# Pooled attention and a softplus FFN on one core: two re-searched instruction orders, and fourteen identity products left out

## The chip, the cores and the metric

The kernel runs on one core of one Trainium2 chip. The metric is the device time of one execution in microseconds (us), as the median of several runs. The kernel of before has a median of 874.52 us over 3 runs (871.99, 874.52 and 875.28).

## What is computed

The reference, cut to what matters. All arrays are float32; B = 8 batches, H = 8 heads, S = 576 positions, D = 64; the FFN has 4608 tokens, 512 inputs and 2048 hidden values.

```python
k_p = k.reshape(B, H, S // 8, 8, D).mean(axis=3)      # keys and values pooled by 8
v_p = v.reshape(B, H, S // 8, 8, D).mean(axis=3)
scores = matmul(q, k_p^T) / sqrt(D);  scores -= max(scores)
attn = exp(scores) / sum(exp(scores))
x = matmul(attn, v_p)                                 # -> 4608 x 512
h = x @ w_in
g = maximum(h, 0) + log1p(exp(-abs(h)))               # softplus
out = g @ w_out
```

## The kernel before

The 4608 tokens are worked on in 18 chunks c of 256. Every float32 factor of the FFN is split into a rounded high part and a low rest, and a product is made of three passes (high by high, high by low, low by high), so TensorE is given three 128x256 products for one.

**Phase 1** (`ORDER1`) holds three chunks (0, 1, 2), the conversion of the 16 blocks of weights on VectorE (`weights`, its last step is L1016), and the pooling of the keys and values of batches 0 and 1 (`batch`). There, `keep_warm` (L313) puts extra products of an identity matrix by itself on TensorE: 3 and 4 in batch 0, 8 ahead of the keys of batch 1 (L1115), and 6 ahead of the transposes of the second q tile of chunk 2 (L360). They write into a bank that is written over afterwards. A 128x128 float32 product shows up as two records.

**Phase 2** (`ORDER2`) holds chunks 3 to 17 in a software pipeline. A chunk has eight blocks u. Steps of one block, with the short names that the text uses:

- **H c.u**: first FFN product, 24 products of 256 columns (L720). TensorE alternates: H c.u, M c.(u-1), H c.(u+1), M c.u, and so on.
- **softplus c.u** on ScalarE (L728), **rounded c.u** on ScalarE (L742), **low c.u** on VectorE (L749).
- From chunk 4 on the second product is made in a scheme of seven products for eight: **sums c.u** are four short operations on VectorE (L782 to L785), **sums-high c.u** on ScalarE (L796), **sums-low c.u** on VectorE (L801).
- **M c.u**: second FFN product, 21 products of 256 columns (L872), three for each of the seven outputs in the order 1, 2, 6, 7, 5, 3, 4. Blocks 0 and 7 have it in two parts of 12 and 9. The seven outputs lie in four PSUM banks, two to a bank; output 4 has half of the fourth bank, and **its three products are the last of every M**: 18 products stand ahead of them.

Steps of the attention of a chunk, which runs two chunks ahead of the FFN: **spread** (eight copies of q on ScalarE, L494), **scores c** (64 small products, L516), then on VectorE **least** (L538) and **less** (L554), on ScalarE **exp c** (L316), on VectorE **expsum** (L1355), **reciprocals** (L1359, L1360), **main** and **ends** (L1363), **turn** (L483), and on TensorE **values c** (L616, L627).

The scores of a chunk need a little more than two banks. From chunk 6 on, the last heads go into the half of the fourth bank of chunk c-2 that no output uses (`third_bank`, `ms[old]["rest"]`). The steps that read this half are called **third least** (L538, 128x144 in) and **third less** (L554, 128x144). They read chunk c's scores while M of chunk c-2 goes on writing output 4 into the other half of the same bank. The list of slots that `pair_scores` and `pair_least` are given names the bank; the M steps have no edge to these two readers in the list of steps.

The order is written out by hand as two lists of numbers of steps. `Order.run` hands out buffers in that order, and the steps are then issued in it: each engine runs its own steps in the order of the list, and where two steps on different engines touch the same tile, the one that stands later in the list waits for the one that stands earlier. ScalarE keeps one table of functions at a time; exponential and softplus are in different ones, and a load (ACT_TABLE_LOAD) stands where the function changes.

Of the kernel before, what the change touches and what calls it, by code (L numbers as in the profile page):

```python
# [69 lines left out]
def pooled_attention_softplus_ffn(  # L70
# [15 lines left out]
    POOL = 8  # L86
    SP = S // POOL
# [262 lines left out]
    def new_E(c):  # L350
        e_[c] = one.tile([P, T, H, SP], F32, tag="E", name="E")

    class Tile:
# [5 lines left out]
        def qT(self, ps):  # L359
            if (self.c, self.t) == (2, 1):  # L360
                keep_warm(ps, 6)
            for m in range(HP):
                nc.tensor.transpose(
                    out=ps[:, m * P:(m + 1) * P],
                    in_=qt_[self.c][:, self.t, 2 * m:2 * m + 2].rearrange("p h d -> p (h d)"),
                    identity=ident)
# [674 lines left out]
    def batch(b):  # L1041
# [60 lines left out]
        for i in range(2):  # L1102
# [10 lines left out]
            def products(i=i, N=N):  # L1113
                if i == 0:
                    keep_warm(bank(s_k, "kps"), (4, 8)[b])  # L1115
                ps = bank(s_k, "kps").rearrange("p (h d) -> p h d", h=H)
                for r in range(N):
                    nc.tensor.matmul(out=ps[0:KM, HP * i:HP * (i + 1)], lhsT=zm,
                                     rhs=x["k", i][:, :, r], start=r == 0, stop=r == N - 1)
            halves.append(op(PE, 0.1 + 0.28 * N, products, [o, *halves], [st[i], s_k]))  # L1120
# [27 lines left out]
    def attend(c):  # L1148
# [16 lines left out]
        for t, x in enumerate(tiles):  # L1165
# [12 lines left out]
            for i, s in enumerate(ss):  # L1178
                d = op(DVE, 0.37, lambda x=x, i=i, s=s, n=s_mn: x.least(i, s.tile, n.name), [p, *ends],
                       [s, s_mn])  # L1180
# [7 lines left out]
                ends.append(op(ACT, 1.18, exp_sum, [d], [s, s_mn, s_sm, s_E], table="exp"))  # L1188
# [153 lines left out]
    def probabilities(c, s_E, s_lt, subs, where):  # L1342
# [4 lines left out]
        if early:  # L1347
            ex = op(ACT, 1.1, lambda: exponential(e_[c]), subs, table="exp")
        else:
            ex = op(ACT, 1.1 + TABLE, lambda: exponential(e_[c]), [*subs, where], s_E)  # L1350
            op(ACT, TABLE, lambda: None, [ex], first=5000)
# [121 lines left out]
    for u in range(U1):  # L1473
# [60 lines left out]
    def first_products(c, u, before):  # L1534
# [16 lines left out]
        else:  # L1551
# [3 lines left out]
               first=HURRY)  # L1555
# [89 lines left out]
    for c in range(N1, NCH + 1):  # L1645
# [166 lines left out]
```

## Time and profile before

| | us |
|---|---|
| median of 3 runs | 874.52 |
| the profiled execution, as timed | 870.77 |
| its span (first to last instruction) | 868.8 |
| TensorE busy | 849.2 (98%) |
| VectorE busy | 661.4 (76%) |
| ScalarE busy | 524.4 (60%) |
| granted TensorE clock, mean | 0.998 |

In the rows, PE is TensorE, DVE VectorE, ACT ScalarE, SP the queue that issues DMAs. A matmul's record covers its way through a pipeline, so two records overlap and a busy PE need not be at its full rate; a row of the timeline gives start, length, and, in square brackets, how long the engine had been idle and what ended that. L numbers are lines of the kernel of before.

### The profile page before, as it was taken

The numbers are of one execution on the slowest core, as the hardware profiler recorded it, in microseconds if no ns is written. First come the engines' busy times: TensorE is split into PE (matmuls) and PEld (weight loads), VectorE is DVE, ScalarE is ACT, GpSimd is POOL, SyncE is SP. The second block draws the span as 40 slices with busy tenths as digits, with TensorE's granted clock in tenths as the row PEclk, the third lists the DMA queues.
The fourth block names the chain that finished last, engine by engine and source line by source line (L and its number), as shares of the span: only waits on it lengthen the run. The fifth ranks groups of instructions, "written<-read, shape, count | busy, mean of one in ns | idle before, by whom it ended". The sixth has DMA issues, their size and how long they took to land.

```text
span 868.8 us, 21296 instructions
## 1 busy us (share of the span) xinstructions
PE 849.2 (98%) x8486; PEld 822.7 (95%) x8486; DVE 661.4 (76%) x1556; ACT 524.4 (60%) x1184; POOL 3.9 (0%) x34
## 2 busy tenths in 40 slices
PE   8999999999999999999999998999999999999997
PEld 5799999999999999899999998999999999999997
DVE  6899999888977877676886787678767765756554
ACT  6843473677875665755874765465755755754532
POOL 1000000000000000000000000000000000000000
PEclk9999999999999999999999999999999999999999
DMA  9668245768999779667787887678866876666772
GB/s 282 204 212 296 101 131 190 245 204 239 333 314 284 243 255 302 225 230 256 251 288 233 287 270 229 216 258 261 276 219 214 267 252 233 203 224 221 250 249 81
DMA packets 117891, 206.91 MB, mean 238 GB/s; under 512 B 47264, under 2 KB 69280, under 8 KB 117792
## 3 DMA queue, kind: packets, MB, share of 16 engines
q1 hardware_dynamic: 117792, 205.55, 72.7%
q8 instruction: 67, 1.10, 0.5%
q14 instruction: 32, 0.26, 0.1%
HBM read 175.11 MB, written 30.41 MB: 237 GB/s over the span
## 4 chain that ended last, share of the span: by engine, by line
PE 54%; ACT 6%; DVE 5%; DMA 1%; issue 1%; SPq 0%; ACTq 0%; DVEq 0%
PE h L720 27%; PE m L872 24%; ACT qT L494 2%; PE avp L616 1%; ACT so L796 1%; PE sc L516 1%; PE avp L627 1%; ACT g L728 1%; DMA out_dram<-o 1%; DMA l<-wi 1%; DVE o L893 1%; DVE so L801 1%; DVE turn L483 1%; ACT gh L742 1%; DVE kst L213 0%
## 5 line engine op out<-in xcount | busy, mean ns | idle before, releaser
L720 PE MATMUL h<-x,l 128*128 128x256 f32 x2748 | 335.3, 278 | 0.6 <-ACT x L636 0.4
L720 PEld LDWEIGHTS h<-x,l 128*128 128x128 f32 x2748 | 323.0, 189 | 2.2 <-ACT x L636 0.8
L728 ACT ACTIVATE g<-h 128x512 f32<-128x512 f32 x120 | 71.9, 599 | 150.0 <-PE h L720 140.8
L872 PE MATMUL m<-w,so 128*128 128x256 f32 x1134 | 149.4, 278 | 1.3 <-DVE o L893 0.8
L872 PEld LDWEIGHTS m<-w,so 128*128 128x128 f32 x1134 | 138.2, 188 | 2.7 <-DVE o L893 1.0
L796 ACT CAST so<-sf 128x512 fp32r<-128x512 f32 x112 | 69.6, 622 | 70.5 <-DVE sf L785 67.6
L494 ACT COPY qT<-turn 32x256 f32<-32x256 f32 x240 | 96.9, 404 | 7.0 <-PE m L516 2.2
L782 DVE TENSOR_TENSOR sf<-g 128x128 f32<-128x128 f32 x112 | 32.0, 286 | 90.3 <-ACT g L728 80.6
L801 DVE TENSOR_TENSOR so<-sf,so 128x512 fp32r<-128x512 f32 x112 | 76.9, 687 | 30.8 <-ACT so L796 28.2
L872 PE MATMUL m<-w,gh 128*128 128x256 f32 x476 | 90.9, 279 | 6.2 <-DVE mn L538 5.0
L749 DVE TENSOR_TENSOR gl<-g,gh 128x384 fp32r<-128x384 f32 (+1 forms) x120 | 67.1, 559 | 19.4 <-ACT gh L742 18.7
L872 PEld LDWEIGHTS m<-w,gh 128*128 128x128 f32 x476 | 72.1, 188 | 6.9 <-DVE mn L538 5.4
L872 PE MATMUL m<-w,gl 128*128 128x256 f32 x238 | 66.7, 280 | 1.1 <-DVE gl L749 0.7
L670 ACT ACTIVATE g<-h 128x256 fp32r<-128x256 f32 x96 | 31.9, 383 | 58.2 <-PE acc L690 38.1
L742 ACT ACTIVATE gh<-h 128x384 fp32r<-128x384 f32 (+1 forms) x120 | 59.4, 495 | 0.4
L665 PE MATMUL h<-x,w 128*128 128x256 f32 x396 | 48.7, 277 | 0.4 <-ACT pT L451 0.4
L665 PEld LDWEIGHTS h<-x,w 128*128 128x128 f32 x396 | 46.6, 188 | 0.8 <-ACT pT L451 0.7
L872 PEld LDWEIGHTS m<-w,gl 128*128 128x128 f32 x238 | 44.8, 188 | 2.3 <-DVE gl L749 2.3
L690 PE MATMUL acc<-w,g 128*128 128x256 f32 x264 | 46.1, 277 | 0.0
L893 DVE TENSOR_TENSOR o<-o,m 128x256 f32<-128x256 f32 x98 | 39.7, 418 | 3.4 <-ACT o L885 0.4
L690 PEld LDWEIGHTS acc<-w,g 128*128 128x128 f32 x264 | 39.8, 188 | 0.0
L872 PE MATMUL m<-l,gh 128*128 128x256 f32 x196 | 37.6, 280 | 1.0 <-DVE E L554 1.0
(211 smaller groups left out, 1331.4 us busy)
## 6 DMA issues: line engine op xcount, KB each, us to landing
l<-wi SPq DMA_DIRECT2D x224, 512.0 KB
out_dram<-o SPq DMA_DIRECT2D x36, 256.0 KB
q<-in_q_dram SPq DMA_DIRECT2D x32, 256.0 KB
moved_p<-turn SPq DMA_DIRECT2D x60, 128.0 KB
pT<-moved_p SPq DMA_DIRECT2D x15, 512.0 KB
kst<-in_k_dram SPq DMA_DIRECT2D x24, 288.0 KB
vst<-in_v_dram SPq DMA_DIRECT2D x24, 256.0 KB
stage<-in_moe_w_in_dram SPq DMA_DIRECT2D x22, 256.0 KB
```

Source lines behind the costliest of these rows:

```text
L494: nc.scalar.copy(out=o, in_=x[a * B32:(a + 1) * B32, s].rearrange("p (u m i) -> p u m i", u=T, i=B32))
L665: nc.tensor.matmul(out=ps[:, 0:CT], lhsT=row(w, kc), rhs=x[:, kc], start=first and kc == j == 0, stop=last and kc == KC - 1 and j == 2)
L690: nc.tensor.matmul(out=accs[c][t][:, ns], lhsT=a[:, ts], rhs=w[:, ns], start=f == 0 and n == j == 0, stop=f == FC - 1 and n == 1 and j == ...
L720: nc.tensor.matmul(out=ps[:, k * CT:(k + 1) * CT], lhsT=row(w, kc), rhs=x_[c][i][:, kc], start=first and n == 0, stop=last and n == len(or ...
L728: nc.scalar.activation(out=g, in_=x.rearrange("p (b i) -> p b i", i=P), func=AF.Softplus)
L742: nc.scalar.activation(out=gh, in_=quarters(c, x.rearrange("p (b i) -> p b i", i=P)), func=AF.Softplus)
L749: nc.vector.tensor_tensor(out=gl, in0=quarters(c, g), in1=gh.bitcast(F32), op=ALU.subtract)
L782: tt(out=sf[:, 2], in0=g[:, 0], in1=g[:, 2], op=ALU.add)
L796: nc.scalar.copy(out=so[:, 0], in_=ss[c, u])
L801: nc.vector.tensor_tensor(out=so[:, 1], in0=sf, in1=so[:, 0].bitcast(F32), op=ALU.subtract)
L872: nc.tensor.matmul(out=ms[c][n], lhsT=x, rhs=y, start=u == 0 and j == 0 and n in (1, 6, 5, 4), stop=u == FP - 1 and j == 2 and n in (2, 7, ...
L893: nc.vector.tensor_tensor(out=o, in0=in0, in1=m[n], op=how)
```

## The change

In the code: the eight identity products ahead of batch 1's keys and the six ahead of the second q tile of chunk 2 are left out; the cost numbers that the order search reads are altered (products of the pooled keys, the exponential of phase 2, which loses its 1.28 us for a table; a step that did nothing but stand for the second table load is gone, 14 of them; softplus steps of phase 2 are marked with their table). `WIDE` is empty, so the steps under it never run. Both lists of numbers are new. Without the marks that cost nothing at run time, the program is the same set of operations less the fourteen products, in another order.

```diff
@@ -84,6 +84,7 @@
+    WIDE = ()
@@ -357,8 +358,6 @@
         def qT(self, ps):
-            if (self.c, self.t) == (2, 1):
-                keep_warm(ps, 6)
             for m in range(HP):
@@ -1111,13 +1110,13 @@
             def products(i=i, N=N):
-                if i == 0:
-                    keep_warm(bank(s_k, "kps"), (4, 8)[b])
+                if i == b == 0:
+                    keep_warm(bank(s_k, "kps"), 4)
...
-            halves.append(op(PE, 0.1 + 0.28 * N, products, [o, *halves], [st[i], s_k]))
+            halves.append(op(PE, 0.1 + 0.45 * N, products, [o, *halves], [st[i], s_k]))
@@ -1347,8 +1359,7 @@
         if early:
             ex = op(ACT, 1.1, lambda: exponential(e_[c]), subs, table="exp")
         else:
-            ex = op(ACT, 1.1 + TABLE, lambda: exponential(e_[c]), [*subs, where], s_E)
-            op(ACT, TABLE, lambda: None, [ex], first=5000)
+            ex = op(ACT, 1.1, lambda: exponential(e_[c]), [*subs, where], s_E, table="exp")
@@ -1474,38 +1485,38 @@
     ORDER1 = [
-        4, 6, 2, 0, 1, 295, 297, 29, 18, 19, 21, 22, 20, 12, 23, 13, 14, 299, 24, 300, 25, 306, 26, 15, 16,
...
+        4, 0, 1, 6, 2, 18, 19, 297, 295, 21, 22, 20, 12, 23, 13, 14, 299, 24, 25, 306, 300, 26, 16, 15, 307,
...
@@ -1552,7 +1563,7 @@
         g = op(ACT, act(2 * CT), lambda: pair_softplus(c, u, s.tile, s_g.name), [o], [s, s_g],
-               first=HURRY)
+               first=HURRY, table="softplus")
@@ -1673,114 +1684,114 @@
     ORDER2 = [
...
```

What the numbers say, step by step, is read out of the two lists with the names above. The function changes on ScalarE are 31 in the list of before and 31 in the list of after (3 in phase 1, 28 in phase 2), besides the one table that is loaded at the start. TensorE's own order in phase 2 is the same but for the places of 9 of the 14 scores steps and of the 5 transposes of the keys, each moved by a few steps. What changes most is how VectorE and ScalarE interleave.

The stretches of the two lists that hold the third least and third less, VectorE's steps and TensorE's steps (in angle brackets) in list order. Before:

```
chunk  8:  ... sums-low 6.4 <M 6.4> <H 6.6> turn less THIRD-LEAST 8, THIRD-LESS 8, rest, sums 6.5 ...
chunk 10:  ... <values 9> low 8.6, turn, sums-low 8.6, pool, av-low, av-low, sums 8.7, THIRD-LESS 10, ... <M 8.6>
chunk 12:  <H 10.3> ... expsum 11, sums 10.3, least 12, THIRD-LEAST 12, reciprocals 11, low 10.3, <M 10.2>
chunk 14:  <H 12.5> ... least 14, less 14, sums 12.5, less 14, turn 15, THIRD-LEAST 14, ... <M 12.4>
```

After:

```
chunk 12:  <H 10.3> <M 10.2> <H 10.4> expsum 11, THIRD-LEAST 12, sums 10.3, reciprocals 11, low 10.3,
           sums-low 10.3, main 11, sums 10.4, ends 11, less 12, turn 11, low 10.4, sums-low 10.4,
           THIRD-LESS 12, ... <M 10.3>
chunk 14:  <scores 14> sums 12.2, sums-low 12.2, low 12.2, THIRD-LEAST 14, least 14, least 14, expsum 13,
           reciprocals 13, main 13, ends 13, <H 12.3> sums 12.3, low 12.3, THIRD-LESS 14, ... <M 12.2>
chunk 15:  <scores 15> sums-low 13.2, <H 13.3> <M 13.2> <H 13.4> least 15, least 15, THIRD-LEAST 15,
           expsum 14, reciprocals 14, main 14, ends 14, sums 13.3, less 15, low 13.3, THIRD-LESS 15,
           less 15, sums-low 13.3, ... <M 13.3>
```

In the chunks that are not listed neither reader stands, in either list, behind the sums of the block whose H is the last one ahead of the next M.

## Rows read from the trace of the kernel before

**Rows 1.** The page, part 1: busy time, share and instructions of each engine.
```profile
PE 849.2 (98%) x8486; PEld 822.7 (95%) x8486; DVE 661.4 (76%) x1556; ACT 524.4 (60%) x1184; POOL 3.9 (0%) x34
```

**Rows 2.** Waits of PE, 50 us to the end: us in total, times, longest.
```profile
PE m L872 <- DVE mn L538: 5.0, 2, 2.7
```

**Rows 3.** Timeline of PE: M steps that start after an idle time.
```profile
356.21 0.50 PE L872 MATMUL m<-w,gh 128*128 128x256 f32 x2 [1.16 <-ACT gh L742]
456.55 0.50 PE L872 MATMUL m<-l,gh 128*128 128x256 f32 x2 [0.98 <-DVE E L554]
526.27 0.51 PE L872 MATMUL m<-w,gh 128*128 128x256 f32 x2 [2.71 <-DVE mn L538]
630.87 0.50 PE L872 MATMUL m<-w,gh 128*128 128x256 f32 x2 [2.28 <-DVE mn L538]
```

**Rows 4.** What VectorE does on the banks of M: ns min/median/max, first and last start.
```profile
L538 DVE TENSOR_REDUCE mn<-m x12: 268/302/310, 260.0 to 766.9; 128x2 f32<-128x144 f32 x12
...
  PE m L872: 4.5, 6
```

**Rows 5.** Timeline: the end of M 6.4, and third least 8 behind it.
```profile
352.06 0.28 PE L872 MATMUL m<-w,gl 128*128 128x256 f32 x1
...
352.37 0.31 DVE L538 TENSOR_REDUCE mn<-m 128x2 f32<-128x144 f32 x1 [2.01 <-PE m L872]
```

**Rows 6.** Timeline: H 10.3, the exponential of chunk 11, the start of M 10.2.
```profile
518.63 2.88 PE L720 MATMUL h<-x,l 128*128 128x256 f32 x24
...
520.42 1.17 ACT L316 ACTIVATE E<-E 128x1152 f32<-128x1152 f32 x1
...
521.35 0.39 PE L872 MATMUL m<-w,gh 128*128 128x256 f32 x2
```

**Rows 7.** Groups of VectorE by shape, 260 to 860 us: busy us, mean ns.
```profile
L801 DVE TENSOR_TENSOR so<-sf,so 128x512 fp32r<-128x512 f32 x106 | 72.8, 687 | 30.5 <-ACT so L796 28.0 <-PE h L720 1.3 <-PE m L872 0.7
L749 DVE TENSOR_TENSOR gl<-g,gh 128x384 fp32r<-128x384 f32 x105 | 57.8, 550 | 19.2 <-ACT gh L742 18.7
...
L1355 DVE TENSOR_REDUCE sm<-E 128x16 f32<-128x1152 f32 x12 | 16.2, 1352 | 9.4 <-ACT E L316 9.3
...
L483 DVE STREAM_TRANSPOSE turn<-pm 128x1024 f32<-128x1024 f32 x12 | 14.9, 1240 | 0.1
L1363 DVE TENSOR_TENSOR pm<-E,sm 128x1024 f32<-128x1024 f32 x12 | 14.6, 1219 | 0.1
```

**Rows 8.** Timeline: the start of M 12.4, the four operations of sums 12.5, the next step.
```profile
626.39 0.39 PE L872 MATMUL m<-w,gh 128*128 128x256 f32 x2
...
628.08 0.29 DVE L782 TENSOR_TENSOR sf<-g 128x128 f32<-128x128 f32 x1 [0.40 <-ACT g L728]
...
629.02 0.45 DVE L554 TENSOR_TENSOR E<-sc,mn 128x288 f32<-128x288 f32 x1
```

**Rows 9.** Stretches: length, PE busy (records), PEld, DVE, ACT, POOL, granted clock, DMA, GB/s.
```profile
527.80:531.20 3.40, 3.40 (x19) 3.40 (x18) 1.69 (x4) 0.05 (x1) 0.00 (x0) 0.50 0.00 0
531.20:534.60 3.40, 3.40 (x32) 3.40 (x32) 2.78 (x7) 2.48 (x5) 0.00 (x0) 1.00 0.92 300
```

**Rows 10.** Timeline of PE: the identity products that the change leaves out.
```profile
17.68 1.95 PE L313 MATMUL kps<-ident 128*128 128x128 f32 x16
...
28.35 1.50 PE L313 MATMUL qTp<-ident 128*128 128x128 f32 x12
```

**Rows 11.** Timeline: ScalarE behind the keys of batch 1, two conversions on VectorE, PE's next H.
```profile
23.76 0.58 ACT L1122 COPY kp<-kps 64x512 f32<-64x512 f32 x1 [2.67 <-PE kps L1118]
...
66.34 2.43 DVE L1016 TENSOR_TENSOR w<-stage,w 128x1024 fp32r<-128x1024 f32 x2
...
67.99 1.18 PE L665 MATMUL h<-x,w 128*128 128x256 f32 x9
```

**Rows 12.** Groups of ScalarE: table loads of phase 2, busy us, mean ns.
```profile
L316 ACT ACT_TABLE_LOAD x15 | 19.2, 1283 | 0.3
L728 ACT ACT_TABLE_LOAD x14 | 18.0, 1283 | 3.3 <-PE h L720 2.9 <-issue 0.3
```

More of the change, by code (lines that the diff above doesn't have):

```diff
@@ L1178, in attend, with less @@
             for i, s in enumerate(ss):
-                d = op(DVE, 0.37, lambda x=x, i=i, s=s, n=s_mn: x.least(i, s.tile, n.name), [p, *ends],
-                       [s, s_mn])
+                d = op(DVE, 0.37, lambda x=x, i=i, s=s, n=s_mn: x.least(i, s.tile, n.name),
+                       [p, *(ends if (c, t) not in WIDE else ())], [s, s_mn])
+                def less(x=x, i=i, s=s, e=s_E):
+                    if c == 0 and 0 not in e_:
+                        new_E(0)
+                    e_[c] = e_[0]
+                    x.slot = e.name
+                    x.less(i, s.tile)
                 def exp_sum(x=x, i=i, s=s, e=s_E, t=t, n=s_sm):
@@ L1187, in exp_sum @@
                     x.exp_sum(i, s.tile, n.name)
-                ends.append(op(ACT, 1.18, exp_sum, [d], [s, s_mn, s_sm, s_E], table="exp"))
+                if (c, t) in WIDE:
+                    ends.append(op(DVE, 0.37, less, [d], [s, s_mn, s_E]))
+                else:
+                    ends.append(op(ACT, 1.18, exp_sum, [d], [s, s_mn, s_sm, s_E], table="exp"))
+            if (c, t) in WIDE:
+                o = op(ACT, act(576), lambda x=x: exponential(e_[c][:, x.t]), ends, [s_E], table="exp")
+                ends = [op(DVE, 0.66, lambda x=x, n=s_sm: x.sum(n.name), [o], [s_E, s_sm])]
             exps.extend(ends)
```

278 rows, old and new, of tables (ORDER1, ORDER2) are left out of this document.

## The prediction

> **What bounds the kernel now.** I read the page's busy shares first: PE is busy 98% of the span [rows 1], so only what makes PE wait, or work that PE no longer has, can count. The pace comes next: the 24 products of an H start at 518.63 and the next M starts at 521.35 [rows 6], 2.72 us for 24, so 0.1134 us a product; an M of 21 is 2.38 us, the 18 products ahead of output 4 are 2.04 us. Then the waits of PE from 50 us on: they are few, and the largest entry names the least of VectorE [rows 2]. In the timeline four waits stand out, 1.16, 0.98, 2.71 and 2.28 us, 7.13 together [rows 3]; no other is over 0.9. Last, what they have in common.
>
> Three of them end with an L538 or L554. Set beside the old list, they are the M steps whose output 4 comes after a third least or third less in the list (chunks 10, 12 and 14), and these readers stand on VectorE behind the sums of the block whose H has only just ended on PE. The other chunks have no reader behind such sums and no such wait: three of three, and none too many. The fourth is the same tie the other way round. Third least 8 sat 2.01 us until M 6.4 was through, its last product starting at 352.06 [rows 5]; the sums behind it were late by that, and so were M 6.5's parts [rows 3]. VectorE waited six times like this, 4.5 us in all [rows 4]. So **the two halves of the fourth bank wait for each other although they share no data**, and a list that has the readers in a bad place pays on PE.
>
> The Trainium skill, PSUM — Partial Sum Buffer, section "PSUM bank collisions raise a hardware error", says that engines are to be kept apart by bank (and quadrant), not by address; by that rule the waits stay in the new list wherever the order makes them, and the trace agrees (2.01 us for a reader whose columns no product wrote [rows 5]); if only the address counted, the sum below would lose the three new waits.
>
> **Part by part. The table switches.** Loads are 1.283 us each [rows 12], and both lists have 31 changes of function, so none is saved. What the new list does is put softplus and its followers behind the exponential with fewer spreads between them. I count other steps between a block's sums and its last rounded part: with the durations of the rows they come to 0.83 us a block on VectorE in the old list and 0.72 in the new one. Waits of PE outside the four are small, about 2 us from 50 us on, each shorter than the shortest of [rows 3]. I take -0.5 us, bounds -2 and +2.
>
> **The bank, in the new list.** Three places, each from the end of the H or M that starts the chain; small steps (ends, less, reciprocals, third readers) at 0.3 [rows 4], sums at 0.94 from start to next start [rows 8], the rest from [rows 7].
> - *M 10.3 waits for third less 12.* From the end of H 10.4: sums 10.4 start 1.7 later (as 12.5 did: 626.39 to 628.08 [rows 8]; at the very least 0.7, the softplus alone), then sums 0.94, ends 0.3, less 0.3, turn 1.24, low 0.55, sums-low 0.69, third less 0.3: 6.0. Records of one engine overlap by some 0.05 each, so 5.6. PE is at output 4 after 2.04: **3.6 us**, bounds 3.0 and 4.0.
> - *M 12.2 waits for third less 14.* Ahead of it on VectorE stand expsum 13 (1.35), reciprocals (0.4), main (1.22), ends 0.3, sums 12.3 (0.94), low 0.55, third less 0.3: 5.1. Exp 13 needs sums-high 12.2, a load (1.28) and itself 1.17 [rows 6, 12]; with H 12.2 ended 6.3 us ahead of H 12.3 it ends about when H 12.3 does. 5.1 less 2.04 is **3.1 us**; if exp 13 comes early and VectorE has done main by then it can fall to 0.5, and reach 3.5.
> - *M 13.3 comes late because third least 15 waits for M 13.2.* VectorE gets to it with M 13.2 still to run (sums-low 13.2 and two leasts are the last work before) and stands, as in [rows 5]. From the end of M 13.2: third least 0.3, expsum 14 1.35, reciprocals 0.4, main 1.22, ends 0.3, sums 13.3 0.94, less 0.4, low 0.55: 5.4. PE is through H 13.4 after 2.72 and wants low 13.3 two products later, at 2.95: 2.4 late, and sums-low 13.3 some 0.6 more: **3.0 us**, bounds 2.4 and 3.5.
>
> Elsewhere the readers have room: in chunks 6, 8 and 10 of the new list a values step or an H lies between. The four old waits go, since their places in the list are gone. So 9.7 (5.9 to 11.0) for 7.13: **+2.6 us**, bounds -1.2 and +3.9. What is queued behind the waiting readers on VectorE are the sums of the next block, and ScalarE and PE wait for these; that is in the sums above.
>
> **The clock.** After the wait of 2.71 us the granted clock was 0.50, the 1.2 GHz level, for 3.4 us: 19 records where the next 3.4 us have 32 [rows 9], 13 products or 1.5 us lost. After the wait of 2.28 us it stayed. Of the three new waits I let two cost this: 3.0 for 1.5, **+1.5 us**, bounds -1.5 (none) and +3.0 (all three).
>
> **The fourteen products.** They are 28 records, 16 in 1.95 us and 12 in 1.50 [rows 10], some 0.11 apart: 3.1 us of PE. PE works without a break around both places, and ScalarE stands 2.67 us until the keys behind the first eight are there [rows 11], so their time is on the path of phase 1's start. But what follows is tied to VectorE: the first of the two conversions that start at 66.34 ends 1.2 us later, and the H that uses it starts at 67.99 [rows 11], 0.4 us on. PE can come earlier there only by as much as VectorE's waits in the head shrink. Half: **-1.5 us**, bounds 0 and -3.1. If the products had kept the clock up, leaving them out would cost; the rows at both places show PE at work before and after, so I take none.
>
> **Sum.** -0.5 + 2.6 + 1.5 - 1.5 = +2.1 us. The profiled execution took 870.77 us around a span of 868.8; on it the change gives 872.9. The runs shown have their median 3.75 above that execution, and I put the difference on the median: 874.52 + 2.1 = **876.6 us**.
>
> **The rivals.** A measurement of this kernel can tell some 0.5% from no change, 4.4 us.
> - *Faster: the readers come in time.* If ScalarE and VectorE run so far ahead in the new list that the third readers are through before PE gets to output 4 (at M 12.2 the 0.5 above; at M 10.3 and M 13.3 the tie would have to be looser than [rows 3, 5] show), the old 7.13 and the 1.5 of the clock go and at most little comes: -7.1 - 1.5 - 1.5 - 0.5 = -10.6, **863.9 us**. For it: the new list keeps softplus directly behind the exponential. Against: third least 15 and third less 12 are behind M 13.2 and sums 10.4 whatever ScalarE does. With half-way cases under -4.4: 24%.
> - *Slower: each bank wait takes the clock with it.* The mechanism is the idle time of PE at M 10.3, M 12.2 and M 13.3; it decides from where each is longer than the 2.28 us after which the clock held. Upper ends: +3.9 + 3.0, and phase 1 gives nothing because VectorE's conversions hold it: +6.9 us, **881.4 us**. For it: all three of my values are above 2.28. Against: the third is in two pieces, and phase 1 should give something. With all over +4.4: 27%.
> - *The change doesn't do what it says.* The number of switches is the same and the fourteen products lie in a stretch tied to VectorE; if the bank waits only trade places, the time stays: **874.5 us**. It is inside the forecast.
>
> **How the numbers follow.** Forecast (within 0.5%, its own range 870.2 to 878.9): 49%, with the third rival in it. Faster 24%, slower 27%. The likeliest case gives 876.6. The range reaches to the ends of both rivals, 863.5 to 882, since cases of both signs hold half of the chance.
>
> **What would show it.** Right: PE waits of some 3 us that end with L554 in the last products of M 10.3 and M 12.2, and one on low (the subtraction of L749) early in M 13.3, with L538 on VectorE idle behind M 13.2; granted clock 0.5 for some 3.4 us behind one or more of them; 32 table loads; PE's first unbroken stretch of H and M one to two us earlier. Wrong: no wait over 1 us on L538 or L554 after 50 us (then the first rival), or phase 1 no earlier, or three stretches of half clock (then the second).

## The result, and the profile after

After takes **865.38 us** (median of 4 runs, 863.49 to 866.56), beside 874.9 us for before on the same chip (4 runs, 871.99 to 875.8). The ratio is 0.9895, with a 95% interval of 0.9865 to 0.9924: 6.7 to 11.8 us faster, 9.5 by the medians. The forecast was 876.6 us and no change. The profiled execution of after took 866.56 us, its span is 864.5 us. Lines from L360 on are one lower in after's code (H is L719, M is L871, less is L553, low is L748).

The page's busy shares first, which answer to [rows 1]. PE is as full as before; it has 28 records fewer, and its busy time is 4.6 us less, of which the products left out make some 3.4 [rows 10].

```profile
span 864.5 us, 21237 instructions
...
PE 844.6 (98%) x8458; PEld 820.2 (95%) x8458; DVE 662.3 (77%) x1556; ACT 522.9 (60%) x1184; POOL 3.9 (0%) x34
```

PE's timeline in after, the three M steps that start or go on after a long idle time (start, length, engine, line, operation; in brackets the idle time and what ended it). They answer to [rows 3]:

```profile
522.79 0.80 PE L871 MATMUL m<-w,gh 128*128 128x256 f32 x2 [3.58 <-DVE E L553]
...
613.25 0.50 PE L871 MATMUL m<-w,gh 128*128 128x256 f32 x2 [2.59 <-DVE E L553]
...
665.53 0.39 PE L871 MATMUL m<-w,gl 128*128 128x256 f32 x1 [2.29 <-DVE gl L748]
```

These are M 10.3, M 12.2 and M 13.3, the three places that the prediction named, with the releasers that it named: third less, third less, low. The idle time of VectorE behind the last one is there too, longer than that of [rows 5]; the timeline of VectorE has third least 15 standing until M 13.2 is through:

```profile
660.33 0.31 DVE L537 TENSOR_REDUCE mn<-m 128x2 f32<-128x144 f32 x1 [3.97 <-PE m L871]
```

Stretches of after (length, PE busy and records, PEld, DVE, ACT, POOL, granted clock, DMA, GB/s), which answer to [rows 9]. Behind M 10.3's wait the clock is at half for 6.8 us, twice as long as in before, and behind M 12.2's for 3.4 us:

```profile
521.60:525.00 3.40, 2.21 (x10) 2.21 (x11) 1.91 (x7) 0.50 (x2) 0.00 (x0) 0.50 0.81 273
525.00:528.40 3.40, 3.40 (x18) 3.40 (x17) 1.25 (x1) 0.00 (x0) 0.00 (x0) 0.50 0.00 0
528.40:531.80 3.40, 3.40 (x32) 3.40 (x32) 1.46 (x5) 2.89 (x9) 0.00 (x0) 0.99 0.81 272
613.80:617.20 3.40, 3.40 (x18) 3.40 (x17) 1.84 (x5) 0.00 (x0) 0.00 (x0) 0.50 0.12 30
617.20:620.60 3.40, 3.40 (x32) 3.40 (x31) 0.99 (x4) 1.97 (x5) 0.00 (x0) 1.00 0.51 154
```

So what the prediction feared happened, and the kernel is still faster. Something else gave back more than it.

**Where it came from.** The view of waits does not show it: outside the long ones it lists for PE, from 50 us on, 2.1 us in before and 1.4 in after. I measured PE from record to record instead. Inside an H or M two records start 0.1134 us apart; what is more than that is lost. A short wait of PE shows up in the view with less than it costs, or not at all, since the records overlap. Here is one in before, the end of H 9.6 and the start of M 9.5:

```profile
491.75 0.50 PE L720 MATMUL h<-x,l 128*128 128x256 f32 x3
492.09 0.39 PE L872 MATMUL m<-w,gh 128*128 128x256 f32 x2
492.82 0.38 PE L872 MATMUL m<-w,gl 128*128 128x256 f32 x1 [0.34 <-DVE gl L749]
```

The third product, the first that needs low, should have started at 492.09 + 2 x 0.1134 = 492.32. It started at 492.82, so 0.50 us are lost where the bracket says 0.34. All such losses under 1 us in the M steps, and what else differs, in the profiled executions of before and after, and of the two with their long waits turned round (flip_before and flip_three, the first experiments):

| | before | after | flip_before | flip_three |
|---|---|---|---|---|
| losses over 1 us in the M steps (us, number) | 7.8, 4 | 9.0, 3 | 1.2, 1 | 1.2, 1 |
| losses under 1 us in the M steps (us, number) | **8.3, 81** | **3.1, 39** | **9.1, 80** | **2.3, 36** |
| lost to half clock ahead of the run's end (us) | 1.6 | 4.1 | 0 | 0 |
| products at 0.118 in place of 0.1134 (us, number) | 3.7, 837 | 2.1, 488 | 4.0, 908 | 1.6, 355 |
| start of chunk 0's first product (us) | 40.27 | 37.72 | 40.32 | 38.24 |
| end of low after the end of its H, mean, 70 blocks behind an exponential (us) | 4.96 | 4.36 | 5.07 | 4.41 |
| of these, later than 5.3 us | **28** | **12** | **31** | **13** |
| the same mean, the other 50 blocks (us) | 3.26 | 3.21 | 3.24 | 3.20 |

The last three rows tell where the largest part of the small losses comes from: at the third and fourth product of an M, which need low, PE loses 3.9 of the 9.1 us in flip_before and 0.8 of the 2.3 in flip_three. "Behind an exponential" means the block whose softplus loads its table again and the four after it. The end of an H is taken where the next product can start, 0.1134 us behind the start of its last one. Low c.u is wanted by the third product of M c.u, and between the end of H c.u and that product PE does M c.(u-1) and H c.(u+1): 2.38 + 2.72 + 0.23 = 5.33 us. In the other 50 blocks low is 2 us early on the mean in both lists. In the 70 it is nearer to the edge: in 28 of them low ends after 5.3 us in before, in 12 in after.

### The profile page after: what moved, and what is told of

Read it like the earlier page. It is cut to its first block, busy times and chain, and to the rows that moved or that the text cites. A ratio compares the mean times of both kernels' runs of the same rounds, so it can differ in the third digit from the quotient of the medians.

```text
span 864.5 us, 21237 instructions
## 1 busy us (share of the span) xinstructions
PE 844.6 (98%) x8458; PEld 820.2 (95%) x8458; DVE 662.3 (77%) x1556; ACT 522.9 (60%) x1184; POOL 3.9 (0%) x34
## 4 chain that ended last, share of the span: by engine, by line
PE 78%; DVE 10%; ACT 6%; DMA 3%; issue 1%; SPq 0%; ACTq 0%; DVEq 0%
PE h L719 31%; PE m L871 26%; PE acc L689 7%; PE h L664 7%; PE avp L615 2%; ACT qT L493 2%; PE avp L626 1%; PE sc L515 1%; DMA kst<-in_k_dram 1%; DMA l<-wi 1%; DVE o L892 1%; PE acc L762 1%; ACT g L727 1%; DVE E L553 1%; DVE gl L748 1%
## 5 line engine op out<-in xcount | busy, mean ns | idle before, releaser
L719 PE MATMUL h<-x,l 128*128 128x256 f32 x2748 | 336.6, 279 | 0.4 <-DMA l<-wi 0.4
L719 PEld LDWEIGHTS h<-x,l 128*128 128x128 f32 x2748 | 324.7, 190 | 1.7 <-DMA l<-wi 0.6
L871 PE MATMUL m<-w,so 128*128 128x256 f32 x1134 | 147.9, 277 | 0.3 <-DVE o L892 0.2
L871 PEld LDWEIGHTS m<-w,so 128*128 128x128 f32 x1134 | 137.3, 188 | 1.0 <-DVE so L800 0.5
L871 PE MATMUL m<-w,gh 128*128 128x256 f32 x476 | 90.5, 278 | 6.2 <-DVE E L553 6.2
L748 DVE TENSOR_TENSOR gl<-g,gh 128x384 fp32r<-128x384 f32 (+1 forms) x120 | 67.0, 558 | 26.0 <-ACT gh L741 25.4
L871 PEld LDWEIGHTS m<-w,gh 128*128 128x128 f32 x476 | 72.0, 188 | 6.6 <-DVE E L553 6.6
L871 PE MATMUL m<-w,gl 128*128 128x256 f32 x238 | 66.2, 278 | 2.4 <-DVE gl L748 2.3
L669 ACT ACTIVATE g<-h 128x256 fp32r<-128x256 f32 (+1 forms) x96 | 32.0, 382 | 57.1 <-PE acc L689 43.9
L871 PEld LDWEIGHTS m<-w,gl 128*128 128x128 f32 x238 | 44.8, 188 | 2.7 <-DVE gl L748 2.7
L871 PE MATMUL m<-l,gh 128*128 128x256 f32 x196 | 37.3, 279 | 0.0
```

The source lines that it names most:

```text
L719: nc.tensor.matmul(out=ps[:, k * CT:(k + 1) * CT], lhsT=row(w, kc), rhs=x_[c][i][:, kc], start=first and n == 0, stop=last and n == len(or ...
L748: nc.vector.tensor_tensor(out=gl, in0=quarters(c, g), in1=gh.bitcast(F32), op=ALU.subtract)
L871: nc.tensor.matmul(out=ms[c][n], lhsT=x, rhs=y, start=u == 0 and j == 0 and n in (1, 6, 5, 4), stop=u == FP - 1 and j == 2 and n in (2, 7, ...
```

## The experiments

The experiments ran on three chips, so each ratio is taken to runs of before on the same chip.

**The long waits, by turning them round.** Which of two steps waits for the other is set by which stands first in the list. In flip_three (from after) and flip_before (from before) every engine keeps its own order, and only that is turned at the three and four places. The edit of flip_three, its list cut to these places:

```diff
 flip_three, second list
-  1216, 1280, 1184, 1284, 1217,            (third less 12, M 10.3)
+  1216, 1217, 1280, 1184, 1284,
-  1515, 1590, 1516, 1517,                  (third less 14, M 12.2)
+  1515, 1517, 1590, 1516,
-  1651, 1658, 1661, 1760, 1764, ... 1758,  (M 13.2, third least 15)
+  1651, 1760, 1764, 1758, 1658, 1661, ...
```

> The kernel after with the order of every single engine unchanged; only which of two instructions comes first in the list is turned round at three places: M 10.3 ahead of third less 12, M 12.2 ahead of third less 14, third least 15 ahead of M 13.2. Theory A (the two halves of the fourth bank wait for each other, and that is all that these three waits are): PE's waits of 3.58, 2.59 and 2.29 us go, the half clock behind them (10.2 us at 0.50, so 5.1 us lost) goes with them, together 13.6 us; as some of it will be late elsewhere, 8 to 13 us below the 865.4 of after, 852 to 857 us. Theory B (PE is behind VectorE and ScalarE there anyway, the wait only shows it): the same waits come a few products later at low, sums-low or the rounded part, and the time stays at 862 to 867 us.

> The kernel before, every engine's order unchanged, with the same turn at its four places: M 10.2 ahead of third least 12, M 12.4 ahead of third least 14, M 8.6 ahead of third less 10, third least 8 ahead of M 6.4. Theory A: its waits of 1.16, 0.98, 2.71 and 2.28 us go, and the 1.5 us of half clock: 5 to 8.5 us below the 874.9 of before, 866 to 870 us, so still above after. Theory B: 873 to 876 us. If the whole gain of the change were in these four waits (a rival to small waits elsewhere), this kernel would be as quick as after with its three waits turned, some 855 us.

Measured: flip_three **853.48 us** (852.91 to 855.17), ratio to before 0.9773 (0.9747 to 0.9799), 11.9 us under after. flip_before **863.95 us** (863.24 to 864.18), ratio 0.9885 (0.9864 to 0.9906), some 10 under before and 1.4 under after. Theory A holds for both: the waits go, and little of them comes back elsewhere. Its time for flip_before, 866 to 870 us and still above after, was missed; the gain was larger. In flip_three PE's waits from 50 us on are

```profile
PE m L871 <- DVE gl L748: 1.4, 2, 1.1
PE avp L615 <- DVE E L553: 0.4, 2, 0.2
PE m L515 <- ACT qT L493: 0.2, 1, 0.2
```

and the mean granted clock of its span is 1.000. Of the 3.58 us at M 10.3, 1.07 come back one M later, at low (PE's timeline):

```profile
526.82 0.39 PE L871 MATMUL m<-w,gh 128*128 128x256 f32 x2
528.28 0.38 PE L871 MATMUL m<-w,gl 128*128 128x256 f32 x1 [1.07 <-DVE gl L748]
```

So the waits and their half clock cost 11.9 us in after and 9.8 in before, by the ratios 10.7 and 10.1. That is +0.6 to +2.1 for the change, which can't be told from nothing. Without them the new kernel is 10.5 us better than the old. flip_three and best_try (below) are the fastest of all and beat both kernels.

**One of the three alone.** flip_first has the first of flip_three's three turns.

> The kernel after with the turn at M 10.3 alone (M 10.3 ahead of third less 12), the other two as they were. In after's profile this wait is 3.58 us and the half clock behind it 6.8 us long, 3.4 us lost: 7.0 of the 11.9 us that the three turns gave, so 858 to 860 us. Rival (the waits overlap: what is not lost there is lost at M 12.2): 861 to 864 us, with the wait at M 12.2 longer than 2.6 us. The prediction's own figures, 3.6 + 1.5 us, would give 860.3 us.

Measured: 863.62 us (861.32 to 868.31), ratio 0.9894 (0.9861 to 0.9927), from which no gain over after can be read. The 858 to 860 us were missed; the time is the rival's, but the longer wait at M 12.2 by which the rival was to show is not there. The profiled execution was the shortest of the four, 861.32 us, 5.2 under that of after; there M 10.3's wait and the 6.8 us of half clock are gone, M 10.4 waits 0.99 us at low, and M 12.2 (2.6) and M 13.3 (2.3) wait as in after. So the waits don't overlap, but what this one is worth stays open.

**The fourteen products and the first list.**

> The kernel after with the fourteen identity products put back (eight ahead of the second batch's keys, six in chunk 2). Forecast of the prediction: they are worth 1.5 us, so 866.9 us. Rival 1 (all of their 3.1 us are on the path): 868.5. Rival 2 (VectorE holds the head anyway): 865.4. Rival 3 (they pay for themselves by keeping the clock up): under 865, with a stretch of granted clock 0.5 in after's first 60 us that is gone here.

> The kernel after with the first list of before (the head and chunks 0 to 2), the second list as in after. In the two profiles the second list starts 2.0 us earlier in after, of which the products should be 1.5: so the first list is worth 0.5 us, and this gives 865.9 us. Rival (the first list is where the search gained): up to 2 us, 867.4 us, with PE's waits in the first 60 us longer by that.

> flip_three (853.5 us) with the fourteen identity products put back. Without the half clock the runs lie closer, and the 1.45 us by which the first product of chunk 0 is late in products_back should be seen at the end: 854.9 us. Rival (the head's gain is lost again in the chunks behind it, as the times of products_back and after say): 853.5 us.

> flip_before (863.95 us) without the fourteen identity products. By first_list_old, whose chunk 0 starts 2.86 us earlier than that of before with the same first list, they are worth 2.8 us with that list: 861.1 us. By the forecast of the prediction 1.5 us: 862.4 us. Rival (nothing is left of it at the end): 864 us.

| | us (range) | ratio to before | start of chunk 0 |
|---|---|---|---|
| products_back | 865.57 (861.77 to 866.94) | 0.9900 (0.9878 to 0.9923) | 39.24 |
| first_list_old | 865.53 (864.05 to 870.66) | 0.9916 (0.9891 to 0.9941) | 37.41 |
| flip_products_back | 855.56 (854.98 to 856.49) | 0.9796 (0.9770 to 0.9821) | 39.39 |
| turned_no_products | 862.77 (860.29 to 867.86) | 0.9885 (0.9852 to 0.9918) | 39.30 |

The runs of each of these four kernels spread over 1.5 to 7.6 us, too wide to choose among the forecasts and their rivals. The third rival of products_back falls: after's profile has no half clock between 7 and 60 us. Chunk 0's first product in the timelines of PE, before, after and products_back:

```profile
40.27 1.43 PE L665 MATMUL h<-x,w 128*128 128x256 f32 x11
```

```profile
37.72 1.43 PE L664 MATMUL h<-x,w 128*128 128x256 f32 x11
```

```profile
39.24 1.42 PE L666 MATMUL h<-x,w 128*128 128x256 f32 x11
```

With the new first list the products put this start off by 1.5 us (39.24 against 37.72), and at the end, where the half clock blurs it less, by 2.1 (855.56 against 853.48, ratios with overlapping intervals). With the old first list they cost 2.9 at the start in one profile (40.27 against 37.41) and 1.0 in another (40.32 against 39.30), in which the clock is at half from 17.3 to 20.7 us, where the products had been. own_first, which has the products, shows the same stretch at 17.6, so that they keep the clock up there is not shown. From the first list itself no gain can be read: 865.53 against 865.38. At the end the products are worth 0.2, 1.2 and 2.1 us in the three pairs of kernels, by the ratios 0.4, 0 and 2.0: 0 to 2 us, and no more can be said.

These runs also give the worth of the two lists by themselves. flip_before and flip_products_back both have the products and neither has a long wait on the fourth bank; between them lie 8.4 us (ratios 0.9885 and 0.9796). Without the products in both, turned_no_products and flip_three, it is 9.3 us (0.9885 and 0.9773).

**The order within a block.** Block 9.5 in the list of before (ScalarE and VectorE) is: softplus, spread, less, less, pooling, spread, rounded, sums, sums-high, pooling, sums-low, low. rounded_first moves rounded behind softplus; rounded_low_first also moves low behind sums; own_first also sums-high and sums-low. All three start from flip_before. For block 9.5:

```
flip_before        softplus, spread, less, less, pooling, spread, rounded, sums, sums-high, pooling, sums-low, low
rounded_first      softplus, rounded, spread, less, less, pooling, spread, sums, sums-high, pooling, sums-low, low
rounded_low_first  softplus, rounded, spread, less, less, pooling, spread, sums, low, sums-high, pooling, sums-low
own_first          softplus, rounded, spread, less, less, pooling, spread, sums, sums-high, low, sums-low, pooling
```

> The kernel before with its four waits turned (flip_before, 863.95 us), and in 60 of its 120 blocks the rounded part moved directly behind its softplus on ScalarE, ahead of the spreads and other steps that its list puts between them. Theory S (the 10.5 us that flip_before is behind flip_three are mostly PE's waits of 0.1 to 1 us inside an M, 9.1 us in flip_before against 2.3, and these come from a rounded part and a low that stand behind other work): the waits fall to 5 or 6 us and the time to 860 to 861.5 us. Theory C (ScalarE and VectorE have no time to spare there, so what is put back makes something else late): 863 to 867 us, the waits of one kind replaced by others.

> rounded_first, and in 69 blocks the low moved on VectorE directly behind the sums, ahead of main, less, least and others. Theory S: PE's small waits fall to 2 or 3 us and the time to 856.5 to 859 us; what then is left to the 853.5 of flip_three are the fourteen products, 2.8 us by the starts of the first product of chunk 0 in the profiles of before and first_list_old. Theory C: not under rounded_first, or slower, because sums-low and the exponential's own steps come later.

> rounded_low_first, and the sums-high (79 blocks) and sums-low (78 blocks) of a block also moved ahead of the other work on ScalarE and VectorE, so that a block's own steps follow each other. In rounded_low_first the waits of PE at low were gone (3.9 us in flip_before at the third and fourth product of an M, 0.1 there) but those at sums-low had grown from 1.5 to 3.9 us. Theory S (what counts is the order within a block): both go, PE's small waits are 1 to 3 us, and the time is 2 to 4 us under rounded_low_first, 858 to 860.5 us. Theory C (VectorE and ScalarE have too much other work in these blocks, whatever stands first; only another share of it among the blocks helps): the waits move to the attention's steps (scores, values, the exponential) and the time is 862 to 868 us.

| | flip_before | rounded_first | rounded_low_first | own_first |
|---|---|---|---|---|
| us | 863.95 | 863.46 | 862.28 | 878.71 |
| ratio to before | 0.9885 | 0.9899 | 0.9883 | 1.0060 |
| losses under 1 us in the M steps (us) | 9.1 | 7.2 | 6.9 | 5.6 |
| of these at low (third and fourth product) | 3.9 | 3.0 | 0.1 | 1.4 |
| and at sums-low (ninth and tenth) | 1.5 | 1.9 | 3.9 | 2.7 |
| end of rounded after its H, the 70 blocks | 3.02 | 1.96 | 2.04 | 2.36 |
| end of low after its H, the 70 blocks | 5.07 | 4.96 | 3.87 | 4.25 |

Theory S, which I had held, falls: its times were missed by all three. Theory C is nearer, in that the waits of one kind were replaced by others, but it also missed the time of own_first (862 to 868 us forecast). With rounded 1.06 us earlier, low is only 0.11 earlier: ScalarE was not what held it. And in the profile of rounded_first the x of the next chunk comes late from ScalarE, a new wait of PE ahead of an H, with half clock for 3.4 us from 814.24 on:

```profile
814.29 4.56 PE L720 MATMUL h<-x,l 128*128 128x256 f32 x24 [2.82 <-ACT x L636]
```

With low ahead of VectorE's other work it is 1.2 us earlier and PE no longer waits for it, but sums-low takes its place. With all of a block's own steps first, the attention is late, and PE waits there, longer. PE's waits in own_first from 50 us on:

```profile
PE avp L616 <- DVE E L554: 6.1, 5, 3.1
PE h L720 <- ACT x L636: 1.9, 2, 1.2
PE sc L516 <- DVE E L554: 1.4, 1, 1.4
```

So changing the order inside the blocks of the old list gained nothing that can be told from noise, and with all of a block's own steps first it lost 15 us. That VectorE has more to do there than the time holds is not borne out for all 70 blocks: from the end of one H to that of the next, it is busy 77, 89, 76 and 59% of the time in the first four blocks behind an exponential in flip_before, and 85, 86, 68 and 63% in flip_three. Only the second block is nearly full. That it helps to give a part of this work to the other 50 blocks, where low is 2 us early, is argued from the two lists; no run moved that work alone.

**The two halves of the second list.** turned_new_then_old is flip_three up to the end of chunk 9 and the old order behind that.

> flip_three with its second list up to the end of chunk 9, and behind that what is left in the order of flip_before's list. In the two profiles 7.2 of the 9.2 us by which PE's steps are longer in flip_before lie ahead of 500 us: so 853.5 + 2.0 = 855.5 us. Rival (the gain up to chunk 9 only comes from work put off): the second half pays it back, 859 to 863 us.

Measured: 859.61 us (857.20 to 861.74), ratio 0.9855 (0.9815 to 0.9896): between both. The 855.5 us were missed, the time is inside the rival's range. Its profiled execution took 857.2 us. The count of late lows goes with it: 20 of the 70, between 13 and 31; its losses under 1 us are 3.8 us, between 2.3 and 9.1. Of the 3.9 us by which its span is longer than that of flip_three, some 2.3 are products at 0.118. One that ought to do better than flip_three:

> flip_three (853.5 us) with the rounded part moved directly behind its softplus in 43 blocks and the low behind the sums in 61. Theory S: the small waits are 2.3 us in flip_three already, so at most 1 to 2 us better, 851.5 to 853.5 us. Theory C: slower, 854 to 858 us.

Measured: 852.54 us (852.20 to 854.61), ratio 0.9780 (0.9745 to 0.9815), which can't be told from flip_three. Its small losses are 1.5 us, and low is late in 5 of the 70 blocks: there was little left to win. One wait of 1.68 us at low and a half clock behind it are new in its profile.

## Why the prediction was wrong, step by step

**The bank waits: right.** Forecast 3.6, 3.1 and 3.0 us, 9.7 in all; measured 3.58, 2.59 and 2.29, 8.46. The 0.6 us that M 13.3 was to lose again at sums-low do not show. For the 7.13 that go [rows 3], that is +1.3 where +2.6 was said. With the half clock the turned kernels give +0.6 to +2.1 for +4.1. The Trainium skill, PSUM — Partial Sum Buffer, section "PSUM bank collisions raise a hardware error", says that the compiler's scheduler adds a dependency between any two instructions on different engines that touch the same bank and quadrant. The runs agree with such a tie: the wait goes in one direction or the other, and the 10 to 12 us hang on the direction alone, which here is set by the order of the list.

**The clock: right in what it does, wrong in how it was put to use.** Two stretches of half clock were forecast, 3.4 us each; there are two, one of them twice as long. The length of a wait does not decide by itself, as the slower rival had it: in products_back (and so in first_list_old) M 12.2 waited 2.08 us and the clock fell, where 2.28 us in before and 2.29 in after left it up (PE's timeline, and the stretch behind it):

```profile
611.31 0.80 PE L873 MATMUL m<-w,gh 128*128 128x256 f32 x2 [2.08 <-DVE E L555]
...
611.40:614.70 3.30, 3.30 (x16) 3.30 (x17) 2.31 (x5) 0.00 (x0) 0.00 (x0) 0.50 0.40 107
```

The larger fault is another one: the difference was put on the median of before as if its other runs were like the profiled one. That one had a mean granted clock of 0.998. Of the 36 runs of before beside the experiments, the 9 at 0.997 to 0.999 have a median of 871.4 us, the 7 at 0.993 to 0.9945 one of 875.5, and the median of all is 873.4 at 0.996. So before too loses the clock more often than its profile shows, and the 3.75 us between the profiled execution and the median fit that: a cost of the old waits, which goes with them (flip_before's four runs are at 0.997 to 1.000). After's four runs lie at 0.993 to 0.995. 0.996 less 0.994 is 0.002 of 865 us, 1.7 us more in after: the +1.5 of the prediction, once it is compared run with run.

**The fourteen products: within the bounds.** -1.5 forecast, 0 to 2 us less measured, in no pair clear of the noise.

**The interleaving: this step failed.** It said -0.5 us, bounds -2 and +2; by the small losses it is -5.1 in the profiles of before and after (8.3 to 3.1 us) and -6.8 in the two turned kernels, and by the times of the two pairs that differ in the lists alone -8.4 and -9.3, in which the products at 0.118 and an earlier chunk 0 are contained. Two things went wrong in it. First, small waits of PE were read from the view of waits, "about 2 us from 50 us on". Taken from record to record they are 8.3 us in the M steps alone. Second, the other steps ahead of low were counted over all blocks, 0.83 us against 0.72, and a mean over 120 blocks hides where they are. By VectorE's records, the work of other steps between sums and low is 48.3 us in the 70 blocks behind an exponential in before and 38.5 in after, while in the others it rises from 17.9 to 22.3. The new list has less of it where low is near the edge and more where there are 2 us to spare. The table loads are 32 in both profiles, as was said. That this share is the cause, and not something else in the new order, is not shown: rounded_low_first took this work away from ahead of low, and its time stayed.

Block 9.5, the one with the 0.50 us above, shows it on ScalarE. Before, whose H ended at 486.99: softplus stands behind four spreads and a conversion, rounded behind two more spreads and three conversions (timeline of ScalarE):

```profile
486.19 1.65 ACT L494 COPY qT<-turn 32x256 f32<-32x256 f32 x4
487.85 0.30 ACT L1326 CAST pm<-pm 128x128 fp32r<-128x128 f32 x1
488.05 0.60 ACT L728 ACTIVATE g<-h 128x512 f32<-128x512 f32 x1
488.67 0.82 ACT L494 COPY qT<-turn 32x256 f32<-32x256 f32 x2
489.51 0.92 ACT L1335 CAST lt__7154<-pm 32x128 fp32r<-32x128 f32 x3
490.44 0.49 ACT L742 ACTIVATE gh<-h 128x384 fp32r<-128x384 f32 x1
```

After, whose H ended at 477.73: rounded directly behind softplus, and on VectorE low ends at 482.74 for a product that starts at 483.31 (timelines of ScalarE, VectorE and PE):

```profile
478.31 0.59 ACT L727 ACTIVATE g<-h 128x512 f32<-128x512 f32 x1
478.80 0.48 ACT L741 ACTIVATE gh<-h 128x384 fp32r<-128x384 f32 x1
...
482.20 0.54 DVE L748 TENSOR_TENSOR gl<-g,gh 128x384 fp32r<-128x384 f32 x1
...
483.07 0.40 PE L871 MATMUL m<-w,gh 128*128 128x256 f32 x2
483.31 0.28 PE L871 MATMUL m<-w,gl 128*128 128x256 f32 x1
```

**The sum.** Between the profiles of before and after the table gives +1.2 (losses over 1 us) + 2.5 (half clock) - 5.2 (small losses) - 1.6 (products at 0.118) - 2.6 (start of chunk 0), or -5.7; the spans differ by -4.3. Between flip_before and flip_three it is -6.8 - 2.4 - 2.1, or -11.3; the spans differ by -11.0. So in the turned pair nearly all of the gain is located, and the small losses are the largest part. Between the medians of before and after lie 9.5 us, 5.3 more than between their profiled executions (870.77 and 866.56): before's profile is one of its faster runs, and after's the slowest of its four.

**The rivals.** The faster one had nearly the right time, 863.9, for a wrong reason: the readers do not come in time. That it was near is luck. The slower one took each bank wait to bring the clock down; M 13.3's 2.29 us did not, as 2.28 had not in before's profile [rows 3, 9].

## What to carry to other kernels

Where an engine is 98% busy, look for its waits from record to record, not in a list of waits, and give each hand-over its time to spare: here low is wanted 5.33 us after its H, and what counts are the blocks in which that time runs short, 28 before and 12 after, not the mean over all blocks. Before a new order is searched, see which waits are only a matter of which step stands first in the list: turning three of them round was worth 11.9 us, the search 9.5. And a difference that was worked out on one profiled execution may only be put on a median if both had the same granted clock.

## What was not expected of the hardware

There are stretches of up to 44 us in which PE's products start 0.1177 us apart in place of 0.1134 though the granted clock is 1.00 in the rows: in before 152 records lie between 235 and 253 us. In the profiles of before, after, flip_before, flip_three and rounded_low_first most of them begin directly behind a step of PE that had lost 0.06 us or more, and end where PE goes over to scores or values, or at another lost step. They cost 1.0 to 5.1 us of a run. So a short wait may cost some 0.5 us more than itself, 130 products at 0.0043, and a part of what the fewer short waits gave may have come in this way. Not every short wait has such a stretch behind it; what decides was not tried.

The half clock lasted 3.4 us in most cases and 6.8 us once, in after at M 10.3; behind the same wait of 3.58 us it lasted 3.4 us in products_back and first_list_old. It also came where no wait over 2 us was left, as in best_try at 529.9 us, behind 1.7 us at low, where flip_three with 1.1 us kept its clock, and in own_first at 430.6 us, behind 1.4 us ahead of scores.
